# One core, pooled attention and a top-1 expert layer: the up products of a block of tokens in another order

## The chip, the cores and the metric

The kernel runs on one core of one Trainium2 chip. The metric is device time in microseconds (us); lower is better. PE is TensorE, ACT is ScalarE, DVE is VectorE, POOL is GpSimd, SP is the engine that issues most of the DMAs.

## The reference, cut to what matters

Attention over keys and values that are averaged in groups of 8 gives 4608 tokens of width 512. Each token then goes to the one of 8 experts that has its largest gate logit, and the result is scaled by the gate's probability:

```python
perm = np.argsort(expert_idx, kind='stable')
x_sorted = x[perm]
boundaries = np.searchsorted(idx_sorted, np.arange(E + 1))
for e in range(E):
    lo, hi = (boundaries[e], boundaries[e + 1])
    h = np.maximum(x_sorted[lo:hi] @ w1[e], 0.0)    # 512 -> 1024
    y_sorted[lo:hi] = h @ w2[e]                     # 1024 -> 512
```

All is in 32-bit floating point. The kernel reaches that with pairs of 16-bit numbers: a value is kept as a high half (its rounding to 16 bits) and a low half (what the rounding left), and a product is the sum of three: high times high, high times low, low times high.

## The kernel before, in words

The first 182 us are attention and routing; tokens are scattered to a buffer that is sorted by expert. After that the expert layer works on blocks of up to 256 tokens of one expert. One block is done ahead of a hardware loop, the others in the loop `for t` (L1323), one per pass. A pass branches (L1332) into one of four copies of `block`: weight slot `s` 0 or 1, and a full block (256 tokens) or a half one (128).

In `block` (L1299) PE first makes the up products. There are 8 pieces `f` of 128 hidden units. `up(s, f, n)` (L1009 and on, matmuls at L1015 to L1017) makes one piece: for each of four slices `d` of the input width, a high weight tile on the high tokens, the same high weight tile on the low tokens, and a low weight tile on the high tokens, 12 matmuls in all, with a weight load (LDWEIGHTS, shown as PEld) before each. So a block has 96 up matmuls. Pieces 2k and 2k+1 share the PSUM bank `pH[k]`: `ps`, `ps`, `pp` and `pq` for k from 0 to 3. When a bank is full, ACT makes the high half of the hidden layer (`relu_hi`, L1086) and DVE the low half (`relu_lo`, L1089). Then `finish` (L1091, matmuls at L1095) multiplies with the second weights: 24 matmuls of 512 columns for each group of 128 tokens, into `pq` for the second group and `po` for the first. `take` (L1256) brings a result out of PSUM on ACT, `give` scatters it to DRAM from POOL.

The weights of the next expert are split in the first block of an expert, in the other weight slot: `part` (L1294) runs `wsplit` eight times behind the relus of that block. Each `wsplit` lets ACT write a high tile (L116) and DVE the low tile made from it (L118). The first four are the first weights, one for each slice `d`; the other four are the second weights. In the trace the tiles of slot 0 are called `w`, those of slot 1 `qt` (first weights) and `kv` (second weights); while slot 0 is filled the loaded weights come from `both`, for slot 1 from `st`. `kv` is also the name of the tile with the transposed tokens `xT`, which `arrive` (L939) fills for the next block. If an expert has only one block, the next block already uses the weights that are still being split.

Each engine executes its own instructions in the order in which they are written. A wait of a weight load on a splitting step of an earlier pass is a wait on a register's value, computed by a REGISTER_ALU instruction ahead of it.

Of the kernel before, what the change touches and what calls it, by code (L numbers as in the profile page):

```python
# [32 lines left out]
def kernel(  # L33
# [10 lines left out]
    nc = tc.nc  # L44
# [5 lines left out]
    DC = Dm // 128  # L50
    FC = F // 128
    assert (H, D, KP, Dm, E, F, N) == (8, 64, 72, 512, 8, 1024, B * S) and S == 576 and B % 2 == 0
    NM = S // 128
    BLK = 256
# [12 lines left out]
    W1 = {}  # L67
# [128 lines left out]
    xT = flat[:, 0:1024].bitcast(F16).rearrange("p (c t) -> p c t", c=2 * DC)  # L196
# [669 lines left out]
    for g in range(NPAIR):  # L866
        u0 = 9 * g
        e, o = 2 * g, 2 * g + 1
        if g:
            for b, at, last in ((e, u0 - 11, u0 - 8), (o, u0 - 7, u0 - 3)):  # L870
                first = 1 if (g == 1 and b == e) else 0
                for f, x in ((pool_k, 0), (pool_v, 2)):
# [6 lines left out]
                    n = 2 * b + x // 2 + 3  # L879
# [46 lines left out]
    def split_x():  # L926
        split_hi()
        split_lo()
# [9 lines left out]
    def arrive():  # L938
        nc.vector.tensor_copy(xT.rearrange("p c (j t) -> p j c t", j=2),  # L939
                              xTs.rearrange("p (j c t) -> p j c t", j=2, c=2 * DC))  # L940
# [67 lines left out]
    pH = []  # L1008

    def up(s, f, n):  # L1010
        dst = pH[f // 2][:, (f % 2) * BLK:(f % 2) * BLK + n]
        c = slice(f * 128, (f + 1) * 128)
        for d in range(DC):
            wh, wl = W1[s][0][:, d, c], W1[s][1][:, d, c]
            nc.tensor.matmul(dst, wh, xT[:, d, 0:n], start=(d == 0), stop=False)  # L1015
            nc.tensor.matmul(dst, wh, xT[:, DC + d, 0:n], start=False, stop=False)  # L1016
            nc.tensor.matmul(dst, wl, xT[:, d, 0:n], start=False, stop=(d == DC - 1))  # L1017

    def up_early(f):
        if not pH:  # L1020
            pH.extend(psA.tile([128, 512], F32, name="ps", bufs=2) for _ in range(2))
        up(0, f, BLK)

    for f, at in enumerate(UPAT):
        put(at, "pe", up_early, f)
# [53 lines left out]
    def pair(x, k, n):  # L1079
        return x[:, 2 * k:2 * k + 2, 0:n]  # L1080

    def ups_of(k, n):
        return pH[k].rearrange("p (f t) -> p f t", f=2)[:, :, 0:n]

    def relu_hi(k, n=BLK):
        nc.scalar.activation(pair(hT[0], k, n), ups_of(k, n), AF.Relu)  # L1086

    def relu_lo(k, n=BLK):
        V.scalar_tensor_tensor(pair(hT[1], k, n), ups_of(k, n), 0.0, pair(hT[0], k, n), op0=OP.max, op1=OP.subtract)  # L1089

    def finish(s, j, half):  # L1091
        y = pY[j]
        for x, z in (((0, 0), (0, 1), (1, 0)), ((0, 0), (1, 0), (0, 1)))[half]:
            for f in range(4 * half, 4 * half + 4):
                nc.tensor.matmul(y, hT[x][:, f, 128 * j:128 * j + 128], W2[s][z][:, f, :],  # L1095
                                 start=(half == x == z == f == 0), stop=(half == z == 1 and f == FC - 1))
# [158 lines left out]
    def take(j):  # L1255
        nc.scalar.activation(ys[j], pY[j], AF.Copy, scale=gB[:, j:j + 1])  # L1256
# [37 lines left out]
    def part(s, en):  # L1294
        with tc.If(en > 0):
            for j in range(8):
                wsplit(1 - s, j, "hl", s)

    def block(s, full, en):  # L1299
        for h in range(2):  # L1300
            n = BLK if full else 128
            for f in range(4 * h, 4 * h + 4):
                up(s, f, n)
            for k in (2 * h, 2 * h + 1):
                relu_hi(k, n)
                relu_lo(k, n)
        arrive()
        split_x()
        part(s, en)
        if full:  # L1310
            for half in range(2):
                finish(s, 1, half)
        take(1)
        for half in range(2):
            finish(s, 0, half)
# [7 lines left out]
    with tc.For_i(0, T, 1, iteration_sync="reg_based") as t:  # L1323
        code = entry(6, t, [ENG.PE, ENG.Activation, ENG.DVE], 0, 3)
        en = entry(2, t, [ENG.Activation, ENG.DVE], 0, 1)
        en3 = [entry(x, t, [ENG.SP], 0, E - 1) for x in (7, 3)]
        more = [entry(5, t + x, [ENG.SP], 0, 1) for x in (2, 3)]
        take_ids()
        move_ids()
        keep_ids()  # L1330
        nc.gpsimd.drain()
        either(code < 2,  # L1332
               lambda: either(code > 0, lambda: block(0, True, en), lambda: block(0, False, en)),
               lambda: either(code > 2, lambda: block(1, True, en), lambda: block(1, False, en)))
        with tc.If(more[0] > 0):
            trans()
        with tc.If(more[1] > 0):
            load_x(t + 3)
        give(1)
        for x in (0, 1):  # L1340
            with tc.If(en3[x] > 0):
                wwhole(en3[x], 1 - x)
        take(0)
        give(0)
# [28 lines left out]
```

## Time and profile before

| | us |
|---|---|
| median of 3 runs | 609.64 (609.46 to 611.69) |
| the profiled execution | 607.49 |
| span of its trace (first to last instruction) | 605.6 |
| PE busy in the span | 567.0 (94%) |
| DVE, ACT, POOL busy | 311.9, 292.2, 268.5 |

The span is the profiled execution without 1.9 us around it. A busy time is a share of the whole span, in which attention and the expert layer have different limits. Matmuls are pipelined and their ends are modelled, so that the start times of matmuls say more than their lengths: the distance of two starts is what one costs. L12 is line 12 of the kernel.

### The profile page before, as it was taken

How to read it: one execution, taken by the hardware profiler on the slowest of the kernel's cores; microseconds unless marked ns; L12 is line 12 of the kernel's file. 1: busy time of each engine (PE TensorE's matmuls, PEld its weight loads, DVE VectorE, ACT ScalarE, POOL GpSimd, SP SyncE). 2: the span in 40 equal slices, each digit the busy share in tenths (PEclk: the TensorE clock that was granted, in tenths of full speed). 3: DMA queues.
4: the chain of work that ended last, by engine and by line, in shares of the span. 5: the costliest groups of instructions: out<-in, count | busy, mean ns of one | idle time of the engine just before them, and what ended most of it. 6: DMA issues, size and time to landing. Idle time of an engine off the chain costs nothing. (4 is left out here: it accounts for less than half of the span.)

```text
span 605.6 us, 15808 instructions
## 1 busy us (share of the span) xinstructions
PE 567.0 (94%) x4727; PEld 418.1 (69%) x4728; DVE 311.9 (52%) x625; ACT 292.2 (48%) x648; POOL 268.5 (44%) x524
## 2 busy tenths in 40 slices
PE   7888989989799989988999999999999899999994
PEld 6777878878686746745676765667756677667762
DVE  6668898987878164117744672324522551223022
ACT  2677889889861262227734552234422641222222
POOL 5698898997886424121351341131421142201212
PEclk9899999999999999999999999999999999999998
DMA  8999798886398549943995879133242323421200
GB/s 241 299 300 269 251 304 272 276 253 220 117 294 243 194 93 336 329 110 97 315 325 126 264 236 315 44 94 80 69 108 46 91 58 93 108 52 37 69 17 33
DMA packets 96404, 107.16 MB, mean 177 GB/s; under 512 B 54446, under 2 KB 64686, under 8 KB 96368
## 3 DMA queue, kind: packets, MB, share of 16 engines
q1 hardware_dynamic: 89808, 86.02, 49.9%
q0 software_dynamic: 6560, 20.69, 9.0%
q8 instruction: 19, 0.31, 0.2%
q14 instruction: 17, 0.14, 0.1%
HBM read 72.99 MB, written 23.37 MB: 159 GB/s over the span
## 5 line engine op out<-in xcount | busy, mean ns | idle before, releaser
L1095 PEld LDWEIGHTS <-bd 128*128 128x128 f16 x936 | 91.3, 98 | 105.6
L1260 POOL TENSOR_TENSOR spacer<-ql,iG 1x1 f32<-1x1 f32 x44 | 22.6, 515 | 195.0 <-ACT ql L1256 192.7
L1089 DVE SCALAR_TENSOR_TENSOR bd<-ps,bd 128x512 f16<-128x512 f32 (+1 forms) x44 | 27.5, 630 | 153.7 <-ACT bd L1086 153.6
L520 ACT ACTIVATE both<-ps,nmx 128x72 f32<-128x72 f32 x288 | 68.5, 330 | 11.8 <-DVE nmx L513 10.4
L1095 PE MATMUL po<-w,bd 128*128 128x512 f16 x264 | 58.9, 379 | 0.0
L1095 PE MATMUL po<-kv,bd 128*128 128x512 f16 x264 | 58.8, 379 | 0.0
L1086 ACT ACTIVATE bd<-ps 128x512 f16<-128x512 f32 (+1 forms) x44 | 24.0, 548 | 67.0 <-PE L1015 47.9
L1261 POOL DMA_INDIRECT out_dram<-ql,iG x44 | 44.5, 1012 | 21.4 <-issue 20.3
L503 PE MATMUL ps<-bd,qT 128*128 128x144 f32 x256 | 45.3, 301 | 3.3 <-ACT both L520 1.8
L1095 PE MATMUL pq<-kv,bd 128*128 128x512 f16 x216 | 48.1, 379 | 0.0
L1015 PE MATMUL ps<-kv,qt 128*128 128x256 f16 (+1 forms) x176 | 44.9, 263 | 1.9 <-issue 1.9
L1017 PE MATMUL ps<-kv,qt 128*128 128x256 f16 (+1 forms) x176 | 44.8, 263 | 1.6 <-DVE qt L118 1.6
L1015 PE MATMUL ps<-kv,w 128*128 128x256 f16 (+1 forms) x176 | 43.1, 258 | 2.8 <-ACT kv L116 2.7
L1016 PE MATMUL ps<-kv,qt 128*128 128x256 f16 (+1 forms) x176 | 44.9, 263 | 0.0
L1017 PE MATMUL ps<-kv,w 128*128 128x256 f16 (+1 forms) x176 | 43.1, 258 | 1.9 <-DVE w L118 1.9
L1016 PE MATMUL ps<-kv,w 128*128 128x256 f16 (+1 forms) x176 | 43.1, 258 | 0.0
L1095 PE MATMUL pq<-w,bd 128*128 128x512 f16 x192 | 42.9, 379 | 0.0
L713 POOL DMA_INDIRECT x_by_expert<-both,rpos x36 | 35.5, 986 | 14.6 <-issue 5.6
L1256 ACT ACTIVATE ql<-po,gB 128x512 f32<-128x512 f32 x22 | 15.1, 684 | 55.3 <-PE L1015 34.5
L1015 PEld LDWEIGHTS <-w 128*128 128x128 f16 x352 | 34.4, 98 | 7.4 <-ACT kv L116 3.2
L1015 PEld LDWEIGHTS <-qt 128*128 128x128 f16 x352 | 34.4, 98 | 7.4 <-issue 2.4
L1017 PEld LDWEIGHTS <-qt 128*128 128x128 f16 x352 | 34.4, 98 | 6.0 <-issue 2.3
(252 smaller groups left out, 1354.0 us busy)
## 6 DMA issues: line engine op xcount, KB each, us to landing
both<-in_moe_w_dram SPq DMA_DIRECT2D x6, 2048.0 KB, 11.2
st<-in_moe_w_dram SPq DMA_DIRECT2D x6, 2048.0 KB, 14.4
vb<-x_by_expert SPq DMA_DIRECT2D x16, 578.0 KB, 5.2
st<-in_moe_w_dram SPq DMA_DIRECT2D x8, 1024.0 KB, 7.2
kv<-in_k_dram SPq DMA_DIRECT2D x7, 1024.0 KB, 8.3
kv<-in_v_dram SPq DMA_DIRECT2D x7, 1024.0 KB, 11.2
qt<-in_q_dram SPq DMA_DIRECT2D x6, 1024.0 KB, 12.2
qt<-in_q_dram SPq DMA_DIRECT2D x4, 512.0 KB, 8.6
```

What stands on the lines that cost most here:

```text
L503: nc.tensor.matmul(ps[:, x * 2 * KP:(x + 1) * 2 * KP], t[:, h, :], BD[b % 3][:, :, h, :], start=True, stop=True)
L520: nc.scalar.activation(p[:, h * KP:(h + 1) * KP], ps[:, x * KP:(x + 1) * KP], AF.Exp, bias=nmx[:, x:x + 1], scale=-1.0)
L713: st = nc.gpsimd.indirect_dma_start(out=xs, out_offset=bass.IndirectOffsetOnAxis(ap=Z["pos"][:, u:u + 1], axis=0), in_=X[:, u, :], in_offs ...
L1015: nc.tensor.matmul(dst, wh, xT[:, d, 0:n], start=(d == 0), stop=False)
L1016: nc.tensor.matmul(dst, wh, xT[:, DC + d, 0:n], start=False, stop=False)
L1017: nc.tensor.matmul(dst, wl, xT[:, d, 0:n], start=False, stop=(d == DC - 1))
L1086: nc.scalar.activation(pair(hT[0], k, n), ups_of(k, n), AF.Relu)
L1089: V.scalar_tensor_tensor(pair(hT[1], k, n), ups_of(k, n), 0.0, pair(hT[0], k, n), op0=OP.max, op1=OP.subtract)
L1095: nc.tensor.matmul(y, hT[x][:, f, 128 * j:128 * j + 128], W2[s][z][:, f, :], start=(half == x == z == f == 0), stop=(half == z == 1 and f ...
L1256: nc.scalar.activation(ys[j], pY[j], AF.Copy, scale=gB[:, j:j + 1])
L1260: nc.gpsimd.tensor_tensor(spacer[:, 0:1], ys[j][0:1, 0:1], iG[0:1, j:j + 1].bitcast(F32), op=OP.add)
L1261: st = nc.gpsimd.indirect_dma_start(out=out, out_offset=bass.IndirectOffsetOnAxis(ap=iG[:, j:j + 1], axis=0), in_=ys[j], in_offset=None, b ...
```

## The change

`block` runs the up products of a block in another order. First the 8 products with the high weight tiles of piece 0, then those of pieces 2, 4 and 6, each in another PSUM bank: 32 matmuls. Then for each bank k: the 4 products with the low weight tiles of piece 2k, the 12 of piece 2k+1 as before, and the two relus. The number of matmuls, of weight loads and of relus is the same, as are the tiles. The block ahead of the loop is not touched.

```diff
+    def up_part(s, f, n, z):
+        dst = pH[f // 2][:, (f % 2) * BLK:(f % 2) * BLK + n]
+        c = slice(f * 128, (f + 1) * 128)
+        for d in range(DC):
+            for x in ((d, DC + d), (d,))[z]:
+                nc.tensor.matmul(dst, W1[s][z][:, d, c], xT[:, x, 0:n], start=(z == 0 and x == 0),
+                                 stop=(z == 1 and d == DC - 1))
 
     def block(s, full, en):
-        for h in range(2):
-            n = BLK if full else 128
-            for f in range(4 * h, 4 * h + 4):
-                up(s, f, n)
-            for k in (2 * h, 2 * h + 1):
-                relu_hi(k, n)
-                relu_lo(k, n)
+        n = BLK if full else 128
+        for f in range(0, FC, 2):
+            up_part(s, f, n, 0)
+        for k in range(4):
+            up_part(s, 2 * k, n, 1)
+            up(s, 2 * k + 1, n)
+            relu_hi(k, n)
+            relu_lo(k, n)
         arrive()
         split_x()
         part(s, en)
```

PE's order at the head of a full block in slot 0, before. `w_00` is the high first weight, `w_01` the low one, and a name behind "waits" is what the instruction waits for (DVE or ACT, of this pass or the one before):

```order
L1015 LDWEIGHTS w_00_60 [waits DVE_I-3729_own,Activation_I-3729_own]
L1015 MATMUL ps<-kv_130,w_00_60 128x256 [waits DVE_49]
L1016 LDWEIGHTS w_00_60
L1016 MATMUL ps<-kv_130,w_00_60 128x256
L1017 REGISTER_ALU
L1017 LDWEIGHTS w_01_61 [waits DVE_I-3729_own]
L1017 MATMUL ps<-kv_130,w_01_61 128x256
L1015 REGISTER_ALU
L1015 LDWEIGHTS w_00_60 [waits Activation_I-3729_own]
```

Before, the third weight load is the low tile of slice 0 and waits for DVE, and a wait for DVE comes with every third matmul until the twelfth.

PE's order at the same place now (`up_part` is L1024):

```order
L1024 LDWEIGHTS w_00_60 [waits DVE_I-3729_own,Activation_I-3729_own]
L1024 MATMUL ps<-kv_130,w_00_60 128x256 [waits DVE_49]
L1024 LDWEIGHTS w_00_60
L1024 MATMUL ps<-kv_130,w_00_60 128x256
L1024 REGISTER_ALU
L1024 LDWEIGHTS w_00_60 [waits Activation_I-3729_own]
L1024 MATMUL ps<-kv_130,w_00_60 128x256
```

Now the third weight load is the high tile of slice 1 and waits for ACT; the fifth and the seventh wait for the high tiles of slices 2 and 3 in the same way.

PE's order in the changed block from the 32nd matmul on, the last one of piece 6:

```order
L1024 MATMUL pq<-kv_130,w_00_60 128x256
L1024 REGISTER_ALU
L1024 LDWEIGHTS w_01_61 [waits DVE_I-3729_own]
L1024 MATMUL ps<-kv_130,w_01_61 128x256
L1024 REGISTER_ALU
L1024 LDWEIGHTS w_01_61 [waits DVE_I-3729_own]
L1024 MATMUL ps<-kv_130,w_01_61 128x256
```

The four waits for DVE now stand ahead of matmuls 33 to 36, one behind the other. The rows of the other engines stand in the same order as before, and PE has as many REGISTER_ALU rows as before.

## Rows read from the trace of the kernel before

**Rows 1.** The page: PE's granted clock in 40 slices, in tenths
```profile
PEclk9899999999999999999999999999999999999998
```

**Rows 2.** Waits of PE from 182 us on: total us, times, longest us
```profile
PE ps L1015 <- ACT kv L116: 2.7, 1, 2.7
...
PE ps L1017 <- DVE w L118: 1.9, 3, 0.6
PE ps L1017 <- DVE qt L118: 1.6, 3, 0.5
```

**Rows 3.** Timeline of PE, block from 279.94: start, length, instruction, idle before
```profile
279.94 0.27 PE L1015 MATMUL ps<-kv,w 128*128 128x256 f16 x1
...
283.62 0.28 PE L1017 MATMUL ps<-kv,w 128*128 128x256 f16 x1 [0.63 <-DVE w L118]
...
292.91 0.38 PE L1095 MATMUL pq<-w,bd 128*128 128x512 f16 x1
```

**Rows 4.** Timeline of PE, block from 480.77
```profile
480.77 0.27 PE L1015 MATMUL ps<-kv,qt 128*128 128x256 f16 x1
...
493.52 0.38 PE L1095 MATMUL pq<-kv,bd 128*128 128x512 f16 x1
```

**Rows 5.** Timeline of PE, full block from 313.81
```profile
313.81 0.27 PE L1015 MATMUL ps<-kv,qt 128*128 128x256 f16 x1
...
324.29 0.38 PE L1095 MATMUL pq<-kv,bd 128*128 128x512 f16 x1
```

**Rows 6.** Timeline of ACT: high tiles of slices 2 and 3, then slice 3
```profile
279.31 1.04 ACT L116 ACTIVATE w<-both 128x1024 f16<-128x1024 f32 x1
280.26 1.04 ACT L116 ACTIVATE w<-both 128x1024 f16<-128x1024 f32 x1
480.79 1.04 ACT L116 ACTIVATE qt<-st 128x1024 f16<-128x1024 f32 x1
```

**Rows 7.** Timeline of DVE: the low tile of slice 3, at both places
```profile
282.34 1.22 DVE L118 SCALAR_TENSOR_TENSOR w<-both,w 128x1024 f16<-128x1024 f32 x1
482.88 1.22 DVE L118 SCALAR_TENSOR_TENSOR qt<-st,qt 128x1024 f16<-128x1024 f32 x1
```

**Rows 8.** Timelines of ACT and DVE: relus of bank 3 in a full block
```profile
211.48 0.60 ACT L1086 ACTIVATE bd<-pq 128x512 f16<-128x512 f32 x1 [2.02 <-PE pq L1017]
212.18 0.69 DVE L1089 SCALAR_TENSOR_TENSOR bd<-pq,bd 128x512 f16<-128x512 f32 x1 [1.92 <-ACT bd L1086]
```

**Rows 9.** Timelines of PE and ACT, half block from 470.23
```profile
470.23 0.22 PE L1015 MATMUL ps<-kv,w 128*128 128x128 f16 x1
473.46 0.38 ACT L1086 ACTIVATE bd<-ps 128x256 f16<-128x256 f32 x1 [0.33 <-PE pp L1015]
475.59 4.70 PE L1095 MATMUL po<-w,bd 128*128 128x512 f16 x21
```

**Rows 10.** Timeline of PE, head of the half block from 268.08
```profile
268.13 0.22 PE L1016 MATMUL ps<-kv,qt 128*128 128x128 f16 x1
268.30 0.22 PE L1017 MATMUL ps<-kv,qt 128*128 128x128 f16 x1
268.52 0.22 PE L1015 MATMUL ps<-kv,qt 128*128 128x128 f16 x1
```

**Rows 11.** Timelines around the switch at 334.65: ACT, ACT, DVE, PE
```profile
328.00 1.06 ACT L921 ACTIVATE bd<-vb 128x1024 f16<-128x1024 f32 x1 [2.75 <-POOL vb L906]
331.80 1.04 ACT L116 ACTIVATE w<-both 128x1024 f16<-128x1024 f32 x1
333.89 1.22 DVE L118 SCALAR_TENSOR_TENSOR w<-both,w 128x1024 f16<-128x1024 f32 x1
334.65 0.27 PE L1015 MATMUL ps<-kv,w 128*128 128x256 f16 x1
```

**Rows 12.** Windows: length, then busy us (count) of PE, PEld, DVE, ACT, POOL, clock, DMA, GB/s
```profile
16.00:24.00 8.00, 7.21 (x54) 6.72 (x54) 6.33 (x14) 5.18 (x20) 4.07 (x5) 0.79 1.09 321
279.90:293.00 13.10, 11.20 (x98) 9.19 (x97) 10.14 (x11) 8.01 (x11) 5.89 (x12) 1.00 0.78 215
```

## The prediction, made before the changed kernel was run

> **What bounds the kernel now.** I read the waits of PE over the expert layer first, then PE's timeline at the places that it names. From 182 us on PE is the engine that sets the pace: its waits that name a source are one of 2.7 us at the loop's second pass, three for DVE's low tiles `w` with 1.9 us and three for `qt` with 1.6 us [rows 2]. The reader is to see that the six waits for DVE belong to two blocks only, and that both are first blocks of an expert whose weights are still being split. The granted clock is full from the first slices on [rows 1].
>
> How much the two blocks lose is not the sum of the listed waits but the distance of starts. An undisturbed full block takes 324.29 - 313.81 = 10.48 us for its 96 up matmuls, 0.109 us each [rows 5]. The block at 279.94 takes 292.91 - 279.94 = 12.97 us, so 2.49 us too much [rows 3]. The block at 480.77 takes 493.52 - 480.77 = 12.75 us, so 2.27 us too much [rows 4]. Together 4.76 us, and that is all that a better order of up products can win here. Both blocks are held until the low tile of slice 3, which DVE ends at 282.34 + 1.22 = 283.56, is there; PE's twelfth matmul follows at 283.62 [rows 3, 7].
>
> **The change part by part.** *The low tiles.* They are now wanted from matmul 33 on, 32 x 0.109 = 3.49 us behind the block's start, and the one of slice 3 at matmul 36. In the first switch that is 279.94 + 3.49 = 283.43 for the first and 283.76 for the last even if nothing else held PE, against 283.56 on DVE; in the second 480.77 + 35 x 0.109 = 484.59 against 482.88 + 1.22 = 484.10 [rows 7]. So the six waits for DVE go, 4.76 us.
>
> *What is late next: the high tiles.* Before, slice 3 was first touched by matmul 10; now by matmul 7, and by then nothing has held PE. In the first switch matmul 7 could start at 279.94 + 6 x 0.109 = 280.59, but ACT ends the high tile of slice 3 at 280.26 + 1.04 = 281.30 [rows 6]. With the 0.06 us that PE needed behind DVE (283.56 to 283.62) it starts at 281.36, 0.77 us late. Slice 2 is ready at 279.31 + 1.04 = 280.35 for matmul 5 at 280.38, which costs 0.03 us at most and lies inside those 0.77. In the second switch matmul 7 could start at 481.42; ACT ends at 480.79 + 1.04 = 481.83, and I give PE 0.15 us behind it, since in that block PE's restart carries waits for more sources: 481.98, 0.56 us late. Behind matmul 7 the next 25 need only high tiles that are there, so the low tiles of the first switch are wanted at 281.36 + 26 x 0.109 = 284.19, 0.63 us behind DVE's end. Net: 2.49 - 0.77 = 1.72 and 2.27 - 0.56 = 1.71, together 3.4 us. The bounds for the price of these two waits are 0 (ACT's tiles are released earlier than its recorded ends) and 0.77 + 0.56 plus a second release of 0.15 each, 1.6 us; so the win lies between 3.1 and 4.76 us.
>
> *The relus.* Bank 0 is full after matmul 48 instead of 24, and then a bank follows every 16 matmuls, 1.75 us instead of 2.62. The two relus take 0.60 and 0.69 us [rows 8], each on its own engine, so 1.75 us hold them. Bank 3 is full after matmul 96 as before, and the relus, `arrive` and the splits behind it stand where they stood. `finish` wants banks 0 and 1 at its start; bank 1 is now full after matmul 64, 32 x 0.109 = 3.49 us earlier, more than 0.60 + 0.69. In the half blocks the room is smaller: 96 matmuls take 475.59 - 470.23 = 5.36 us, 0.056 each, so bank 1 is full 1.79 us ahead of `finish`. The relu of bank 1 began at 473.46 when matmul 48 had started at 470.23 + 47 x 0.056 = 472.86, 0.60 us behind it, and takes 0.38 [rows 9]; now matmul 64 starts at 473.76, the relu ends near 474.74, 0.85 us before `finish` at 475.59. I cost this at nothing. If that cover were gone, each of the five half blocks (10 of the 44 relus on `ps` are of the half form, two to a block) would pay what the relu is late, at most its 0.38 us: 1.9 us.
>
> *The waits that stand together.* Four REGISTER_ALU rows with a wait now stand ahead of four matmuls in a row. What such a row costs when PE's instruction stream has run dry shows at the half block from 268.08: the step to the next matmul is 0.17 or 0.22 us with the row [rows 10], 0.056 without. Before, seven such rows stood ahead of the first ten or twelve matmuls of every block, and in all blocks but the one just named and the two switches they cost nothing visible: the undisturbed full block is an even 0.109 us per matmul from end to end. The stream runs ahead while PE does the 512-column products. Now three of the seven stand there and four come later, when the stream has had 24 matmuls to get ahead again. I take 0, with 0 and 0.17 x 4 = 0.68 us per block as ends.
>
> *What the saved time meets.* Everything behind the switches hangs on PE, except where ACT waits for tokens that a DMA brings. At the switch at 334.65 ACT's splits begin behind a wait of 2.75 us for POOL, which waits for that load [rows 11]. If the load does not come earlier, PE arrives 1.72 us sooner, at 332.93, and wants slice 3's high tile at 333.58; ACT ends it at 331.80 + 1.04 = 332.84. It wants the low one at 332.93 + 3.82 = 336.75; DVE ends it at 333.89 + 1.22 = 335.11. So the first win survives this place in the new order.
>
> **Sum.** The profiled execution took 607.49 us, its span 605.6. It becomes 607.49 - 3.4 = 604.1. The median of the three runs lies 2.15 us higher than the profiled execution, for which I know no cause in the program, so the forecast for the median is 609.64 - 3.4 = **606.2 us**, 0.56% less. That is close to 0.5%, about what a measurement of this kernel can tell from no change, which is 606.6.
>
> **The rivals.** *The win of one switch is given back.* A load that comes when it came before makes PE wait later for what it won at 279.94; the wait of 2.75 us for POOL [rows 11] is for it, the 0.7 us and 1.6 us of room just worked out are against it, as is that PE shows no other wait for a source. The time: 609.64 - 1.7 = 607.9.
>
> *ACT's tiles do not hold PE at all.* If PE's restart does not follow ACT's recorded end, the whole 4.76 us are won: 604.9. Against it: PE's restarts followed DVE's ends by 0.06 us.
>
> *Slower: the four waits in a row drain PE's instruction stream in every block.* In a full block four such matmuls would take 4 x 0.22 instead of 4 x 0.109 us, 0.44 us more; there are 16 full blocks in the loop, so 7.0 us. In the five half blocks it is 4 x 0.17 = 0.68, 3.4 us. Together 10.4 us less the 3.4 won: 609.64 + 7.0 = 616.6. It makes the kernel slower as soon as a third of that cost shows. For it: the steps of 0.17 and 0.22 us [rows 10]. Against it: the even blocks in which seven such rows stand closer to the block's start.
>
> *Slower: the clock falls.* This trace has a stretch with a granted clock of 0.79 (16 to 24 us), that is partly at 1.2 instead of 2.4 GHz [rows 12]; at 1.2 GHz an up phase of 10.48 us would take 10.48 us more, and if that came at each of the two switches the kernel would take 609.64 - 3.4 + 21 = 627. Against it: the stretch of the first switch had clock 1.00 with PE busy 11.20 of 13.10 us and three stops in it [rows 12], and the new order leaves one stop. The Trainium skill (TensorE: Matmul & The Clock Gate, section A second HAM failure mode: psum-queue depth-cycling) tells of a kernel that cycled through PSUM banks and in which small idle pieces between groups of matmuls made the clock swing between its levels; the new order does go through four banks at the head of each block, and by that rule this rival would be the outcome. The rows do not bear it out: PE already goes through four banks per block at full clock.
>
> **How the numbers follow.** The forecast (both waits for DVE gone, one short wait for ACT in each switch) gets 0.66, with a range of its own of 605.2 to 607.2: the win's bounds of 3.1 and 4.76 us and 0.4 us for the scatter of medians. The win half given back gets 0.19, the whole win 0.07, the drained stream 0.07, the clock 0.01. The range from 604.4 (the whole win and 0.5 us) to 609.2 takes in the given-back win and most of a forecast that is spoiled by late relus (1.9 us), and leaves out the slower cases and a change that does nothing. Faster by over 0.5% is time under 606.6: the whole win's 0.07 and about 0.50 of the forecast's 0.66, so 0.57. Slower is 0.08. The rest, 0.35, is no change.
>
> **What would show it.** In PE's waits of the changed kernel the six entries for DVE's `w` and `qt` tiles are gone, and there are two for ACT's L116 instead, about 0.5 and 0.7 us, ahead of each block's seventh matmul. The two up phases take about 11.2 and 11.0 us, all other full ones 10.5 and the half ones 5.4. The forecast is wrong if an undisturbed block takes more than 10.5 us with steps of 0.2 us at matmuls 33 to 36, if `finish` waits for a relu in a half block, if a new wait appears between the two switches, or if the clock leaves 1.00.

## The result, and the profile after

The changed kernel takes 604.83 us (median of 6 runs, 604.25 to 607.88) against 610.94 us for the kernel before in the same session (median of 6, 609.46 to 611.85). The ratio is 0.991, with a 95% interval of 0.9885 to 0.9935: 4.0 to 7.0 us less. Over all sessions of this study (a session is a set of runs taken together) the medians are 608.85 us for the kernel before (87 runs, 605.9 to 616.1) and 605.27 us for the changed one (30 runs, 603.3 to 609.7), 3.6 us apart. The profiled execution took 604.97 us, its span is 602.3 us, 3.3 us less than the span before.

PE's waits from 182 us on in the changed kernel: total us, times, longest us.

```profile
PE ps L1024 <- DVE qt L118: 2.3, 1, 2.3
PE ps L1024 <- issue: 2.2, 1, 2.2
PE ps L1024 <- ACT qt L116: 0.4, 1, 0.4
PE ps L1024 <- ACT w L116: 0.3, 1, 0.3
```

The three waits for `w` and the three for `qt` of [rows 2] are gone. What took their place are the two last lines, one wait for ACT in each of the two switches that lost time (a switch is a block that starts on newly split weights). The first line is the stop at the loop's second pass, which was there before with 2.7 us and another name; the second is the stop ahead of the half block, 1.90 us before.

The first switch, PE's timeline: start, length, instruction, idle time before it. One row stands for neighbouring matmuls of one line into one tile.

```profile
280.38 0.82 PE L1024 MATMUL ps<-kv,w 128*128 128x256 f16 x6
281.48 1.27 PE L1024 MATMUL ps<-kv,w 128*128 128x256 f16 x10 [0.28 <-ACT w L116]
282.58 1.04 PE L1024 MATMUL pp<-kv,w 128*128 128x256 f16 x8
283.45 1.04 PE L1024 MATMUL pq<-kv,w 128*128 128x256 f16 x8
284.32 0.60 PE L1024 MATMUL ps<-kv,w 128*128 128x256 f16 x4
284.76 0.27 PE L1015 MATMUL ps<-kv,w 128*128 128x256 f16 x1
...
291.31 0.38 PE L1103 MATMUL pq<-w,bd 128*128 128x512 f16 x1
```

The stop sits ahead of the seventh matmul, as forecast. The up phase (the 96 up matmuls of a block) takes 291.31 - 280.38 = 10.93 us, against 12.97 [rows 3]. The eight matmuls ahead of the four low products take 284.32 - 283.45 = 0.87 us and the four, with their computed waits, 284.76 - 284.32 = 0.44 us, 0.109 each: nothing drains there.

The second switch, PE's timeline:

```profile
479.17 0.82 PE L1024 MATMUL ps<-kv,qt 128*128 128x256 f16 x6
480.38 1.25 PE L1024 MATMUL ps<-kv,qt 128*128 128x256 f16 x10 [0.40 <-ACT qt L116]
...
490.21 0.38 PE L1103 MATMUL pq<-kv,bd 128*128 128x512 f16 x1
```

It takes 11.04 us, against 12.75 [rows 4]. The high tiles of slice 3 on ACT and the low one of the first switch on DVE, which answer to [rows 6, 7]:

```profile
280.38 1.04 ACT L116 ACTIVATE w<-both 128x1024 f16<-128x1024 f32 x1
479.20 1.04 ACT L116 ACTIVATE qt<-st 128x1024 f16<-128x1024 f32 x1
282.46 1.22 DVE L118 SCALAR_TENSOR_TENSOR w<-both,w 128x1024 f16<-128x1024 f32 x1
```

PE goes on 0.06 us behind ACT's end in the first switch (281.42 to 281.48) and 0.14 us in the second (480.24 to 480.38). DVE's last low tile of the first weights is there at 283.68, before matmul 33 at 284.32 asks for the first of them.

An undisturbed full block takes 322.69 - 312.21 = 10.48 us, as before [rows 5], so the other blocks win nothing by the new order:

```profile
312.21 1.91 PE L1024 MATMUL ps<-kv,qt 128*128 128x256 f16 x16
...
322.69 0.38 PE L1103 MATMUL pq<-kv,bd 128*128 128x512 f16 x1
```

Where the 3.3 us of span come from, by PE's starts: the two up phases give 2.04 and 1.71 us, the stretch up to the second pass 0.59, the half block 0.92 (5.76 instead of 6.68 us). The stop ahead of the half block took 0.32 us more, and the second pass 1.63 more: its 96 matmuls took 12.11 us instead of 10.48. Together 5.26 - 1.95 = 3.31. Why the second pass was slower the windows show (length, busy us and count of PE, PEld, DVE, ACT, POOL, clock, DMA, GB/s):

```profile
223.70:227.10 3.40, 3.37 (x16) 2.42 (x17) 3.40 (x4) 3.37 (x5) 0.46 (x1) 0.50 0.15 35
227.10:236.00 8.90, 8.90 (x82) 7.95 (x81) 3.92 (x5) 1.79 (x3) 5.43 (x12) 1.00 0.87 285
```

For 3.4 us behind the stop at the second pass the granted clock was 0.50, that is 1.2 GHz, and 16 matmuls took what 31 take at 2.4 GHz. In the profile before the clock was full there. It changes from run to run: of the 13 profiles of this study nine have such a slow second pass (12.1 us), `before_swap` in the old order among them, and four have not, `again` in the new order among them.

### The profile page after: what moved, and what is told of

It is laid out like the page before. It is cut to its first block, busy times and chain, and to the rows that moved or that the text cites. A ratio compares the mean times of both kernels' runs of the same rounds, so it can differ in the third digit from the quotient of the medians.

```text
span 602.3 us, 15808 instructions
## 1 busy us (share of the span) xinstructions
PE 567.2 (94%) x4727; PEld 419.6 (70%) x4728; DVE 312.0 (52%) x625; ACT 292.3 (49%) x648; POOL 267.9 (44%) x524
## 4 chain that ended last, share of the span: by engine, by line
PE 67%; DVE 11%; ACT 11%; DMA 5%; issue 3%; POOL 2%; SPq 1%; ACTq 0%; POOLq 0%; DVEq 0%; PEld 0%
PE po L1103 16%; PE pq L1103 14%; PE ps L1024 8%; ACT both L520 4%; PE pq L1024 4%; PE pp L1024 4%; DMA qt<-in_q_dram 3%; PE ps L1015 3%; PE ps L1017 3%; PE ps L1016 3%; DVE vb L450 2%; ACT ph L532 2%; DVE pl L538 2%; PE pp L1015 2%; PE pp L1016 2%
## 5 line engine op out<-in xcount | busy, mean ns | idle before, releaser
L520 ACT ACTIVATE both<-ps,nmx 128x72 f32<-128x72 f32 x288 | 68.5, 330 | 11.8 <-DVE nmx L513 10.4
L1024 PEld LDWEIGHTS <-qt 128*128 128x128 f16 x528 | 48.0, 98 | 10.7 <-issue 3.5
L1024 PEld LDWEIGHTS <-w 128*128 128x128 f16 x480 | 42.2, 100 | 10.2 <-ACT kv L116 2.8
L503 PEld LDWEIGHTS ps<-bd,qT 128*128 128x128 f32 x256 | 34.8, 190 | 4.7 <-ACT both L520 2.2
L924 DVE TENSOR_TENSOR bd<-vb,bd 128x1024 f16<-128x1024 f32 x22 | 27.0, 1226 | 17.8 <-issue 7.4
L1264 ACT ACTIVATE ql<-pq,gB 128x512 f32<-128x512 f32 x22 | 15.0, 682 | 42.6 <-PE pq L1103 40.4
L327 POOL TENSOR_TENSOR st<-kv 128x1280 f32<-128x1280 f32 x12 | 34.8, 2902 | 0.2 <-issue 0.2
L538 DVE SCALAR_TENSOR_TENSOR pl<-pp,ph 128x640 f16<-128x640 f32 x36 | 29.5, 820 | 10.3 <-ACT ph L532 10.3
L1024 PE MATMUL ps<-kv,qt 128*128 128x256 f16 (+1 forms) x264 | 32.2, 263 | 2.7 <-issue 2.2
L513 DVE TENSOR_REDUCE nmx<-ps 128x4 f32<-128x288 f32 x72 | 32.3, 449 | 3.6 <-PE ps L503 3.5
```

Source lines behind the costliest of these rows:

```text
L327: nc.gpsimd.tensor_tensor(t1, src[:, :, 0:4 * D], src[:, :, 4 * D:], op=OP.add)
L503: nc.tensor.matmul(ps[:, x * 2 * KP:(x + 1) * 2 * KP], t[:, h, :], BD[b % 3][:, :, h, :], start=True, stop=True)
L513: nc.vector.tensor_reduce(nmx, ps[:, 0:4 * KP].rearrange("p (h x) -> p h x", x=KP), axis=AX.X, op=OP.min)
L520: nc.scalar.activation(p[:, h * KP:(h + 1) * KP], ps[:, x * KP:(x + 1) * KP], AF.Exp, bias=nmx[:, x:x + 1], scale=-1.0)
L538: nc.vector.scalar_tensor_tensor(pl, pp[:, 0:640], SP, ph, op0=OP.mult, op1=OP.subtract)
L1024: nc.tensor.matmul(dst, W1[s][z][:, d, c], xT[:, x, 0:n], start=(z == 0 and x == 0), stop=(z == 1 and d == DC - 1))
```

## The experiments

The theory: PE lost 4.76 us in the two switches because DVE's low tiles were late, and the new order wins this back but for a short wait for ACT. The main rivals: the win comes from the heads of all blocks (fewer computed waits among the first matmuls), or from the order of the banks and the later relus; and, for what is left between 3.4 us and the first measured 6.1, the clock.

**The changed kernel again** (`again` and `again2`, unchanged, beside the others).

> The changed kernel once more, beside the others. Theory (the six waits for DVE's low tiles were the gain, 3.75 us in the two switches, plus 0.9 us at the head of the starved half block): 3.5 to 5.5 us under the kernel before; up phases of the two switches 10.9 and 11.0 us; the half block at 269 near 5.8 us. Rival (the clock): the rest of the measured 6.1 us is where the granted clock happens to fall to 1.2 GHz in the loop's second pass or in the half block at 269; then this run's profile shows that stretch at another place or not at all, and with it 1.6 us more or less.

> The changed kernel beside the next one on the same chip: 3.5 to 4.5 us less than the kernel before; switch up phases 10.8 to 10.9 and 11.0 us.

Measured: 605.11 us against 608.67 (ratio 0.9929, 0.9901 to 0.9958) and 605.45 against 608.46 (0.9959, 0.9933 to 0.9985), so 3.6 and 3.0 us less, the second below the 3.5 that were expected at least. The switches take 10.75 and 11.03, 10.93 and 11.04 us. In the first of the two profiles the clock in the second pass is full and its up phase takes 10.48 us, in the second it is 0.50 again and takes 12.14. The half block near 269 takes 7.60 and 5.74 us. So the switches repeat to 0.2 us, while the second pass and the half block change by 1.7 and 1.9 us between runs of one and the same kernel. The 0.92 us that the half block gave in the first pair of profiles cannot be counted as a gain of the change: in `again` it takes longer than in the kernel before.

**Piece 0 as before, the rest of the new order** (`piece0`).

```diff
-        for f in range(0, FC, 2):
+        up(s, 0, n)
+        for f in (2, 4, 6):
             up_part(s, f, n, 0)
         for k in range(4):
-            up_part(s, 2 * k, n, 1)
+            if k:
+                up_part(s, 2 * k, n, 1)
             up(s, 2 * k + 1, n)
```

> Piece 0 is made as before (low products among its high ones), and only then the high products of pieces 2, 4 and 6; banks and relus come in the order of the changed kernel. Theory: all six waits for DVE are back, up phases near 12.9 and 12.7 us, the half block at 268 near 6.7 us: the time of the kernel before within 1 us. Rival (the order of banks and the later relus bring the gain): the time of the changed kernel.

Measured: 608.34 us, ratio 0.998 (0.9947 to 1.0012). PE's waits from 200 us on:

```profile
PE ps L1015 <- issue: 3.6, 1, 3.6
PE ps L1015 <- ACT kv L116: 2.3, 1, 2.3
PE ps L1017 <- DVE qt L118: 1.6, 3, 0.5
PE ps L1017 <- DVE w L118: 1.5, 3, 0.6
```

All six waits for DVE are back, the up phases take 12.52 and 12.76 us, and the gain is gone. Banks and relus come in the order of the changed kernel here, so they bring nothing that shows.

**Fewer pieces ahead** (`dose2`: pieces 0 and 2; `dose3`: 0, 2 and 4). The edit for `dose2`; `dose3` has `(0, 2, 4)` and `k < 3`:

```diff
-        for f in range(0, FC, 2):
+        for f in (0, 2):
             up_part(s, f, n, 0)
         for k in range(4):
-            up_part(s, 2 * k, n, 1)
+            if k < 2:
+                up_part(s, 2 * k, n, 1)
+            else:
+                up(s, 2 * k, n)
             up(s, 2 * k + 1, n)
```

> Only pieces 0 and 2 have their high products first, 16 instead of 32 matmuls. Theory: the low tile of slice 3 is wanted 0.56 + 19 x 0.109 = 2.6 us behind the block's start, DVE has it 3.3 us behind it: a wait for DVE of about 0.7 us comes back in each switch (up phases near 11.7 us), about 1.5 us more than the changed kernel. Rival (the gain comes from the heads of all blocks, where the computed waits for DVE no longer stand among the first matmuls): the same as the changed kernel within 0.3 us, since these waits are gone from the head here too.

> Pieces 0, 2 and 4 have their high products first, 24 matmuls instead of 16 or 32. Theory (only the time at which the low tile of slice 3 is wanted counts): it is wanted 0.5 + 27 x 0.109 = 3.4 us behind the block's start, DVE has it 3.3 to 3.4 us behind it in the second switch and earlier in the first; so at most 0.1 us of wait for DVE, switch up phases of 10.8 to 11.0 and 11.0 to 11.2 us, the time of the changed kernel within 0.3 us. Rival (the count of banks is what helps, each of the four as much as the other): halfway between 16 and 32 matmuls, up phases near 11.2 and 11.4 us.

Measured: `dose2` 608.94 us (ratio 0.9996, 0.9964 to 1.0028), switches 11.59 and 11.88 us; `dose3` 604.98 us against 608.46 (0.9948, 0.9924 to 0.9972), switches 10.81 and 11.04 us. The second switch of `dose2` on PE's timeline:

```profile
483.87 0.82 PE L1024 MATMUL ps<-kv,qt 128*128 128x256 f16 x6
485.08 1.58 PE L1024 MATMUL ps<-kv,qt 128*128 128x256 f16 x13 [0.40 <-ACT qt L116]
487.35 0.27 PE L1024 MATMUL ps<-kv,qt 128*128 128x256 f16 x1 [0.69 <-DVE qt L118]
```

The wait for DVE is back in one piece of 0.69 us (0.67 in the first switch), as worked out, ahead of the twentieth matmul, the one with the low tile of slice 3. With 24 matmuls ahead it is gone. Over 0, 2, 3 and 4 pieces the first switch takes 12.97, 11.59, 10.81 and 10.93 us and the second 12.75, 11.88, 11.04 and 11.04: the win ends where the low tile is no longer asked for before it is there, and the fourth piece adds nothing. The median of `dose2` is 3.8 us above that of `again` in the same session, where 1.5 were expected. Its 12 runs have a mean granted clock of 0.990, those of `again` 0.992, so a part of that may be the clock. Its profile also has the 1.2 GHz stretch at the second pass and again in the half block (7.54 us); whether more than chance brought these on was not settled.

**The slice as the outer loop** (`dmajor`, and twice more as `dmajor2`, `dmajor3`). The high tile of slice 3 is then asked for at matmul 25.

```diff
-        for f in range(0, FC, 2):
-            up_part(s, f, n, 0)
+        for d in range(DC):
+            for f in range(0, FC, 2):
+                dst = pH[f // 2][:, 0:n]
+                for x in (d, DC + d):
+                    nc.tensor.matmul(dst, W1[s][0][:, d, f * 128:(f + 1) * 128], xT[:, x, 0:n], start=(x == 0), stop=False)
```

> High products of pieces 0, 2, 4, 6 with the slice as the outer loop, so that the high tile of slice 3 is wanted at matmul 25 instead of 7. Theory: the two waits for ACT (0.28 and 0.40 us of idle, 0.45 and 0.56 us of up phase) go too; both switch up phases 10.5 us, 1.0 us less in all than the changed kernel, none of the 9 other blocks slower. Rival (ACT's waits are hidden or the stream bounds the head): same time as the changed kernel within 0.3 us.

> The slice-outer order once more, for a closer interval. Theory: 4.76 us of switch excess gone against 3.75 to 3.94 in the changed kernel, so 0.8 to 1.0 us less than the changed kernel and 4 to 5 us less than the kernel before. Rival: the times of both are the same.

> The slice-outer order beside the changed kernel: both switch up phases 10.5 us, 0.8 to 1.0 us less than the changed kernel, 4.5 to 5.5 us less than the kernel before. Rival (what is won at the switches is given back at the next wait for tokens): the time of the changed kernel.

Measured: 604.67 us (ratio 0.9937, 0.9906 to 0.9967), 603.9 against 609.21 (0.9883, 0.984 to 0.9925), 604.79 against 608.46 (0.9931, 0.9906 to 0.9956). The second switch of `dmajor`, PE's timeline:

```profile
479.57 0.60 PE L1313 MATMUL ps<-kv,qt 128*128 128x256 f16 x4
...
490.05 0.38 PE L1103 MATMUL pq<-kv,bd 128*128 128x512 f16 x1
```

All six switches of the three profiles take 10.47 or 10.48 us: the wait for ACT is gone, and with it the last of the 4.76 us. Over the three sessions the median is 604.34 us (25 runs), 0.9 us under the changed kernel's 605.27, and 4.5 under the kernel before. Beside the changed kernel in the same session it is 0.4 (`dmajor`) and 0.7 us (`dmajor3`) lower, where 0.8 to 1.0 were expected. The intervals against the kernel before overlap, so the times alone do not settle that it beats the changed kernel; the traces do show the two waits gone. A part is given back: in two of the three profiles PE starts the block near 313 late by 0.33 and 0.57 us. In the profile of `dmajor3`, the one with 0.33 us, ACT's split of the tokens ahead of that block waited for POOL, whose tokens come by DMA:

```profile
312.21 1.06 ACT L921 ACTIVATE bd<-vb 128x1024 f16<-128x1024 f32 x1 [3.01 <-POOL vb L906]
```

It ends at 313.27, PE starts at 313.57, 0.30 us behind. In `dmajor2` PE starts 0.30 us behind the end of the same split too (312.88 and 313.18), and there its wait is listed against ACT's queue at L1303, the branch of `part` behind the split. That the load of tokens is the cause is read from these waits; it was not tested. The kernel before had this block start right behind the one ahead of it [rows 5].

**The low tiles earlier, in the old order** (`xlo_late`). DVE makes the low half of the next tokens behind the four splits of the first weights. The edit is cut: `part` is also given the list of the splits that it runs.

```diff
         arrive()
-        split_x()
-        part(s, en)
+        split_hi()
+        part(s, en, range(4))
+        split_lo()
+        part(s, en, range(4, 8))
```

> The kernel before (old order of up products), with one edit on DVE: the low half of the next block's tokens (L924, 1.22 us) is made behind the four splits of the first weights instead of ahead of them, so that the low tiles come 1.14 us earlier. Theory (PE stood still because DVE's low tiles were late): the up phases of the two switches shrink by 1.1 us each, to about 11.8 and 11.6 us, 2.2 us less in all than the kernel before, with the order of the matmuls untouched. Rival (something in the order of the up products itself, banks or computed waits, cost the time): both up phases stay at 12.97 and 12.75 us.

Measured: 616.12 us against 609.21, ratio 1.0104 (1.0073 to 1.0135). The first switch takes 15.10 us instead of 12.97, and the second 12.61, 0.14 less than before and not 1.1. The switch at 340.81, which lost nothing before, takes 12.49 us, with three waits for DVE again. ACT and DVE ahead of the second switch:

```profile
486.13 3.88 ACT L116 ACTIVATE qt<-st 128x1024 f16<-128x1024 f32 x4
```

```profile
487.49 4.63 DVE L118 SCALAR_TENSOR_TENSOR qt<-st,qt 128x1024 f16<-128x1024 f32 x4 [1.47 <-ACT qt L116]
```

DVE had nothing else to do and still could not begin: a low tile is made from the high one, and ACT ends the first high tile at 487.17. The low tiles began 1.45 us ahead of the block instead of 1.30 (479.47 against 480.77 before), 0.15 us earlier, and the up phase shrank by 0.14. So the premise of this edit was wrong, DVE's work on the tokens lay in time that it had to wait anyway; its size agrees with the theory but is too small to be a test of it, and the first switch says nothing on it, since there the splits themselves began later, behind a wait for tokens. And it cost 7 us, which the trace lays to the tokens: the transposing DMA of the tokens waits for their low half, the next load of tokens is issued behind it on SP (at 261.56 instead of 256.76 us), and ACT's split of tokens then waited 10.8 and 3.4 us for POOL.

**The half copy of the slot 1 block nearer in the program** (`before_swap` in the old order, `dmajor_swap` with the slice as the outer loop).

```diff
-               lambda: either(code > 2, lambda: block(1, True, en), lambda: block(1, False, en)))
+               lambda: either(code < 3, lambda: block(1, False, en), lambda: block(1, True, en)))
```

> The kernel before, with the half and the full copy of the slot 1 block exchanged in the program, so that the half one stands directly behind the slot 0 copies. Theory on the scatter (PE's instructions for the half block of slot 1 are fetched only when it is first entered, near 265 us; PE waits for that fetch, and the clock may fall to 1.2 GHz behind the stop): the stop of 1.9 us or more ahead of the block near 268 and the 0.4 to 3.8 us inside it become shorter or move to the first full block of slot 1 near 314; 2 to 4 us less if the fetch then comes in time. Rival (the stop is a wait for tokens or for another engine): stop and block as before.

> The slice-outer order of high products together with the exchanged copies of the slot 1 block. If both theories hold, the two switches have up phases of 10.5 us and the stop ahead of the block near 268 is shorter: 5 to 8 us less than the kernel before, 1 to 4 us less than the changed kernel. If the stop has another cause, the time of the slice-outer order alone, 4 to 5 us less than the kernel before.

Measured: 609.3 us (ratio 1.0003, 0.9976 to 1.0029) and 604.39 us (0.9897, 0.986 to 0.9935). In `before_swap` the stop ahead of the half block is gone (0.0 instead of 2.07 us between the last product and it), none shows ahead of the first full block of slot 1 (315.24) either, and the half block takes 5.36 us instead of 6.68. But nothing is won:

```profile
276.92 1.06 ACT L921 ACTIVATE bd<-vb 128x1024 f16<-128x1024 f32 x1 [3.08 <-POOL vb L906]
```

```profile
278.99 0.28 PE L1015 MATMUL ps<-kv,w 128*128 128x256 f16 x1 [0.95 <-ACT w L116]
```

ACT waits 3.08 us for the tokens and splits the next weights later than PE wants them; PE stands 0.95 us ahead of the first switch, and its up phase takes 15.35 us, with a stretch of 3.4 us at 1.2 GHz in it (granted clock 0.50 from 282.7 to 286.1). So the stop at the half block is hidden behind the load of tokens, which bounds the first switch when PE comes earlier. `dmajor_swap` shows no gain over the slice-outer order alone (604.39 against the 603.9 us of `dmajor2` in that session), and its first switch takes 11.77 us where 10.5 were expected: ACT's split of the tokens waits 2.27 us for POOL there, the splits of the weights come behind it, and PE waits 0.85 us for DVE's last low tile at matmul 36. Its second switch takes 10.48 us. That the stop went when the copy was moved fits a late arrival of PE's instructions; which part of the supply is late was not tried.

## Why the prediction was right, step by step

*The six waits for DVE go.* Right: none is left, and `piece0` brings all six back with the whole time.

*The high tile of slice 3 is late next.* Right in place, ahead of matmul 7, in both switches. The forecast was 0.56 us in the second, and its up phase is 11.04 - 10.48 = 0.56 too long. In the first it was 0.77, and 0.45 was measured: PE went on 0.06 us behind ACT as assumed, but the high tile came earlier relative to the block, its step beginning with the block (280.38) and not 0.32 us behind it [rows 3, 6]. ACT's split of the tokens, behind which the splits of the weights stand, began after a wait of 0.26 us there, and of 0.76 before. So the switches gave 3.75 us where 3.43 were forecast. That size is luck in part: it hangs on when PE arrives, and in `again` the first switch is 0.27 us too long and not 0.45.

*The relus cost nothing.* Right: no half block but the one with the stop takes more than 5.36 us, `finish` starts without a listed wait everywhere, and `piece0`, with the same relu order, stays at the old time.

*The four computed waits in a row cost nothing.* Right: steps of 0.109 us at matmuls 33 to 36, and 10.48 us for each undisturbed full block. PE's queue runs the seven register rows of the full block from 353.89 between 352.5 and 355.8, the last of them well ahead of matmul 36 near 357.7, so that the stream had not run dry. The rival that would have made the kernel slower is refuted. Its cost was also put too high: in a half block the step of 0.17 us replaces one of 0.056, so four rows cost 0.46 us and not 0.68, and five blocks 2.3 us; the rival's sum is then 9.3 us and not 10.4.

*The win is kept to the end.* Right for the changed kernel: from the first switch to the second, and from there to the end, every block starts as much earlier as the switch gave. But the room at the switch from 334.65 was smaller than worked out. The prediction let ACT's splits come there when they came before and got 0.74 us between the high tile of slice 3 and matmul 7. In the changed kernel ACT's split of the tokens waited 4.83 us for POOL instead of 2.75 and began later, at 328.48 instead of 328.00 [rows 11]; the tile ended at 333.33, 0.37 us ahead of matmul 7. In `again` nothing was left:

```profile
329.59 1.06 ACT L921 ACTIVATE bd<-vb 128x1024 f16<-128x1024 f32 x1 [5.25 <-POOL vb L906]
333.40 1.04 ACT L116 ACTIVATE w<-both 128x1024 f16<-128x1024 f32 x1
333.75 0.27 PE L1024 MATMUL ps<-kv,w 128*128 128x256 f16 x1
```

There the tile ended at 334.44, PE could have started matmul 7 at 333.75 + 6 x 0.109 = 334.40, and with the 0.06 us behind ACT's end it is 0.10 us late: that block takes 10.58 us. In `dmajor`, which brings PE another 0.5 us forward, the wait for tokens takes 0.3 to 0.6 us back near 313, so the limit named by that rival is near.

*The clock.* The rival put the fall at the switches, and there the changed kernel's clock is full, 1.00 in both up phases. It does fall in the second pass, to 0.50 behind a stop of 2.3 us that the change did not make. So one of the prediction's own signs of being wrong, that the clock leaves 1.00, did come, at a place that it had not named; it comes in both orders, and cost 1.63 us in this profile. A fall at the first switch is on record too, but in the old order, in a profile where PE stopped longer there (`before_swap`, stops of 0.95 and 1.31 us ahead of it). Between the two switches (291.31 to 479.17) the blocks of the new order go through four banks twice each, PE has no listed wait, and the granted clock is 1.00. The Trainium skill (TensorE: Matmul & The Clock Gate, section A second HAM failure mode: psum-queue depth-cycling) tells of a kernel in which small idle pieces came with the cycling through PSUM banks and the clock went up and down. Here the cycling came without such pieces, and by itself it did not bring the clock down.

*The size.* Forecast 3.4 us, pooled medians 3.6 us apart. The measured 604.83 us lies in the prediction's whole range but below the forecast's own (605.2 to 607.2), and next to the 604.9 of the rival in which ACT's tiles do not hold PE. The time alone would have spoken for that rival; the two waits for ACT ahead of the seventh matmul refute it. The forecast's own range also does not follow from the terms named for it: 609.64 less 3.1 to 4.76 us, with 0.4 us on either side, is 604.5 to 606.9.

The first session's 6.1 us is the top of a scatter that the prediction met as 2.15 us between the profiled execution and the median, without a cause. Now it has one, in part: the 35 runs of the kernel before in one session go from 606.2 to 615.3 us, and their mean granted clock and their time go against each other with a correlation of -0.85. Two places differ from profile to profile: the second pass (10.48 or 12.1 us) and the half block of slot 1 with the stop ahead of it (7.8 to 11.4 us in all in the orders without the exchange). The order does not show in the clock: in two sessions its mean is 0.9921 and 0.9918 over the runs of the changed kernel, 0.9922 and 0.9919 over those of the kernel before. And runs of like clock keep the difference: among those with a mean granted clock of 0.995 or more, 26 of the kernel before have a median of 607.41 us and 8 of the changed one 603.80, 3.6 us apart. That the spans of the first two profiles differ by 3.31 us, close to the forecast, is luck in part, since beside the 3.75 us of the switches 1.51 us were won and 1.95 lost at places that change from run to run. What decides in which runs the clock falls stays open, and so does the rest of the first session's 6.1 us; its runs of the kernel before have no clock on record.

## What to carry to other kernels

When an engine works with operands that two others still prepare one behind the other, order its work by when each operand arrives: first all that needs the early ones, over as many accumulators as there are banks, with the loop over the arriving slices outermost. Work out from the trace how much such work is needed ahead (here 24 matmuls were enough, 16 were not) and look at once at the operand that is late next. A stop elsewhere that looks free to remove may lie over a load that bounds the next step; see what waits behind it before counting it.

## What the runs showed of the hardware that was not expected

A stretch of 3.4 us with a granted clock of 0.50 behind a stop of PE of 2.3 us cost 1.63 us in one profile, and did not come in another profile of the same kernel behind a stop of nearly the same length (2.74 us between the last product and the next block, against 2.48). Over the 13 profiles the listed stops ahead of a second pass with the fall are 2.17 to 2.78 us, and those without it 1.18, 1.88, 2.58 and 2.69 us, so the length of the stop alone does not decide. PE went on 0.06 us behind the end of ACT's or DVE's tile in one copy of the block and 0.14 to 0.15 us in the other. In the changed kernel PE's queue has ten EVENT_SEMAPHORE rows of 51 ns for the head of the second switch (slot 1) and one for that of the first (slot 0). That these rows are the difference was not tested.
